# A new written-out order for five engines, and other queues for three early loads, in a fused spectral-filter and MLP kernel

## The chip, the cores and the metric

The kernel runs on one core of a Trainium2 chip. The metric is the device time of one execution in microseconds (us), lower is better. The profile is of one execution of the kernel before the change.

## What is computed

The input x is 2048 rows of 640 bf16 values. It is normalised along its rows (mean and variance, no scale), and two branches work on the normalised xn; their results are added to x.

```python
xn = (x - mean(x)) / sqrt(var(x) + 1e-5)
A  = irfft2(rfft2(xn) * (w_r + 1j * w_i))            # 2048 x 640
B  = gelu(xn @ w1 + b1) @ w2 + b2                    # 640 -> 1536 -> 640
out = x + A + B
```

Branch A is done with matrix products against cosine and sine tables; branch B is two dense layers. Both are work for TensorE.

## The kernel before

**Tiling.** The 2048 rows are 16 chunks of 128. Chunks are normalised one by one: two statistics instructions each on VectorE (line 651), their aggregation (653), the power -0.5 on GpSimd (655), the subtract-and-scale on VectorE (673). A normalised chunk is needed twice. Transposed, it is the right-hand side of the first dense layer: chunks 0 to 3 are transposed by TensorE against an identity matrix (692) and copied out of PSUM, chunks 4 to 15 by a DMA transpose issued by SyncE (680). Folded (two chunks at a time, "a pair": lines 704 and 708, VectorE), it is the left-hand side of the first spectral step, five matmuls a chunk against the table `gtab` (line 715), whose result is copied to `XV` (720) by ScalarE or VectorE.

**First dense layer.** The rows are taken in seven blocks, `BLOCKS = [(0, 1), (1, 1), (2, 2), (4, 2), (6, 2), (8, 4), (12, 4)]` (first chunk, number of chunks). For each block there are 12 slices of the hidden width, each of five matmuls (128 columns of x per chunk of the block), issued as a group of three and a group of two (lines 736 to 739), then one GELU on ScalarE (742) that empties the PSUM bank. W1 comes in three parts by slices, `W1P = [(0, 3), (3, 7), (7, 12)]`: slices 0 to 2, 3 to 6, 7 to 11. So a slice of block 1 with number 8 can only start when the third part of W1 has landed.

**The rest.** Then come the spectral steps B (against `etab`), C (`mtab`), the filter products on VectorE (809, 813), D (`ntab`), a DMA transpose back (834), E (`getab`) and the last step against `htab` (918) that is added into the same PSUM bank as the second dense layer (899), VectorE's addition of x (920) and the store (923). The second dense layer is 12 times 640 columns per chunk. For the chunks in `KEEP` it is done early and set aside by an addition on VectorE (911); for the others late. x and b2 are brought together in SBUF by a copy on ScalarE (887) and an accumulating DMA of GpSimd (905). All these matmuls are issued by the helper at line 536, so the profile tells them apart by tile names: `ps<-xnT,W` is the first dense layer, `ps<-W,gT` the second, `ps<-gtab,T` the first spectral step, `ps<-warm` matmuls on zeros that are issued to keep TensorE busy (42 at the start, 12 more later; `WARM`).

**Order.** The operations are numbered in the order in which the source creates them, and `ORDER` holds, for each engine (`sp`, `pe`, `act`, `dve`, `pool`), the list of its operations in the order in which it issues them. An engine runs its list strictly in order and waits at each entry for the semaphores of what that entry reads. `schedule()` walks the lists with a model of durations and of DMA landing times; with the lists given, what it decides is the PSUM bank or SBUF slot of each buffer, by the modelled times. For a DMA it computes a landing time:

```python
331  done = max(t + ring.lead, free[e] - dur + ring.lead, dma_free) + n * ROW_NS[size] / 1e3
338  o.end = done + TAIL + (LAG if 8.0 < t < 60.0 and o.engs[0][0] != "pool" and size != 256 else 0.0)
```

PSUM has eight banks. First-layer slices use banks 4 to 7, steps B, C, D and E use 0 to 3, the first spectral step takes three free banks of all.

**The loads at the start**, in the source:

```python
585  load_x(0, 1)
586  load(ident[:], const["I"], B_id, (8, 256), q="pool", prio=96, late=1.25)
587  load_x(1, 1)
588  load(b1t[:], b1v, B_b1, (1, 256), q="act", prio=410)
589  load_w1(0, q="act")
590  K.op([("act", 1.3)], 390, lambda e, _: e.preload_act_table(ACT.Gelu_apprx_tanh), ...)
591  load_w1(1)
592  load_x(2, 2)
593  load_w1(2)
```

**Numbers that the text uses** (the list entry, before / after, where the two differ because the start of the source or the number of copies at line 720 differs):

| operation | number before | number after |
|---|---|---|
| load of identity, of b1, of W1 part 0 | 9, 11, 12 | 10, 11, 13 |
| table load on ScalarE | 13 | 9 |
| load of x chunk 0, of x chunk 1 | 8, 10 | 8, 12 |
| W1 part 1, x chunks 2 and 3, W1 part 2, `gtab` | 14, 15, 16, 17 | the same |
| x chunks 4-5, 6-7, 8-9, 10-11, 12-13, 14-15 | 18, 19, 20, 24, 25, 28 | the same |
| b2, `getab` | 27, 50 | the same |
| W2 quarter 0, quarter 2, `mtab` | 23, 29, 32 | the same |
| DMA transposes of chunks 4 to 11 | 149 151 162 164 175 177 188 190 | the same |
| block 1 slice 8, first group | 290 | 289 |
| first spectral step of chunks 4 and 5 | 158, 159 | 158, 159 |
| first slice of block 3 (chunks 4 and 5) in the list | 353 | 343 |
| first part of the second layer, chunk 0 | 605 | 604 |

Of the kernel before, what the change touches and what calls it, by code (L numbers as in the profile page):

```python
# [9 lines left out]
ACT = mybir.ActivationFunctionType  # L10
# [77 lines left out]
HOLD = 0.3  # L88


def mm_us(n):
    return max(n / 2400.0 + 0.0027, 0.0265)

# [23 lines left out]
class Pool:  # L117
# [31 lines left out]


ORDER = {
    "sp": """8 10 14 15 16 17 18 27 50 46 24 20 19 25 23 149 151 30 45 162 164 42 28 29 38 175 177 31 188 190 36 32
26 37 33 40 41 39 217 47 34 48 49 44 219 202 43 204 35 521 522 523 520 544 545 546 51 547 570 568 569 571 595 594
593 592 621 658 648 638 612 694 675 710 720 685 730 756 765 747 782 798 791 805""",
    "pe": """7 52 112 114 115 236 230 231 120 233 118 237 234 245 246 248 249 275 276 284 285 269 270 278 279 239 242 243 240 272 266 273
# [8 lines left out]
728 760 761 754 762 745 763 785 786 787 780 792 793 788 789 794 795 796 799 800 801 802 803""",  # L164
    "act": """11 12 13 53 116 232 121 238 235 247 250 277 286 271 280 244 241 274 268 292 256 253 134 137 283 301 265 130 328 131 322 307
# [3 lines left out]
566 563 574 573 587 457 460 466 478 475 463 469 757 597 598 481 472 624 783 748 660 661 696 732 733 767""",  # L169
    "dve": """0 54 55 56 59 58 111 60 113 117 122 123 119 66 63 62 65 64 67 124 126 125 132 135 127 138 139 69 70 72 73 71  # L170
# [5 lines left out]
662 664 665 697 698 693 699 779 701 700 674 735 768 734 709 736 737 719 769 684 770 729 772 755 771 764 746 781 790 797 804""",  # L176
    "pool": """3 1 2 9 4 57 61 68 75 82 89 96 5 103 22 21 6 110 604 630 677 650 739 640 667 774 712 722 614 784 749 758
687 703""",
}


# [17 lines left out]

ROW_NS = {256: 26, 384: 22, 512: 27, 640: 33, 642: 70, 768: 37, 1024: 47, 1280: 56, 1600: 68, 2560: 103, 4096: 160, 10272: 750, "acc": 152}  # L200
TAIL = 0.9
LAG = 1.6


LAT = {"pe": 0.2, "dve": 0.125, "act": 0.16, "pool": 0.12}
# [2 lines left out]
class Sched:  # L208
# [37 lines left out]

    def schedule(self):
        free = {e: 0.75 for e in self.engines}
        dma_free = 0.0
# [29 lines left out]
        while left:  # L279
            best = None  # L280
            for e in self.engines:
                cands = []
                for o in [p for p in pend[e] if p is fixed[e][len(self.order[e])]] if fixed and len(self.order[e]) < len(fixed[e]) else pend[e]:
# [17 lines left out]
                    t = max(r, free[e])  # L301
# [7 lines left out]
                t0 = min(c[0] for c in cands)  # L309
# [3 lines left out]
                t, o = min(near, key=lambda c: (-c[1].prio, c[1].seq))  # L313
# [13 lines left out]
            if o.nbytes:  # L327
                n, size = o.rows
                ring = rings[e]
                free[e] = ring.issue_end(t, dur, n)  # L330
                done = max(t + ring.lead, free[e] - dur + ring.lead, dma_free) + n * ROW_NS[size] / 1e3
                if e == "pool" and size == 256:
                    done = t + ring.lead + 0.6
                    dma_free += n * ROW_NS[size] / 1e3
                else:
                    dma_free = done
                ring.held.append((done, n))
                o.end = done + TAIL + (LAG if 8.0 < t < 60.0 and o.engs[0][0] != "pool" and size != 256 else 0.0)
            else:
                o.end = t + dur + LAT[e]  # L340
            for b in o.writes:
# [60 lines left out]
    def emit(self, es, last):  # L402
# [40 lines left out]
PRIO = {"hps": 30.0, "gelu": 46.5, "pb": 53.0, "pc": 64.0, "filt": 77.5, "ipc": 53.5, "eps": 47.0, "fin": 46.5}  # L443
AHEAD = 1
# [4 lines left out]
FOLD = (1.3, 1.8, -3.7, 28.8, -1.2, 39.3, 36.8, -1.2)  # L449
GP = (-43.0, 20.0, 8.0, 14.0, -28.0, 2.0, -14.0)  # L450
G1 = 0
WAVE = (0, 4, 0, 0, 0, 1, 0, 4, 2, 2, 3, 0, 2, 1, 1, 2)
WARM = (42, 12)


def bass_parallel_sum__spectral_gfnet__dense_activation_gelu__prompt_kernel(
# [12 lines left out]
    const = {k: nc.inline_tensor(_bf16_bits(v.reshape(128, -1)), name=f"c_{k}").ap().bitcast(BF) for k, v in T.items()}  # L469
# [4 lines left out]
    b1v = B_b1.rearrange("(c p) -> c p", p=128)  # L474
    b2v = B_b2.rearrange("(o e) -> o e", o=1)

    K = Sched(nc, ["sp", "pe", "act", "dve", "pool"])
    with ExitStack() as es:
# [11 lines left out]
        ident = sb("ident", [128, 128])  # L490
# [7 lines left out]
        b1t = sb("b1t", [NFC, 128])  # L498
# [31 lines left out]
        def load(dst, src, buf, rows, after=(), q="sp", issue=0.46, prio=400, gate=(), late=0.0):  # L530
            return K.op([(q, 0.7 if q == "pool" else issue)], prio, lambda e, _: e.dma_start(dst, src), writes=[buf], after=after, rows=rows, gate=gate, late=late)  # L531
# [35 lines left out]
        B_id, B_b1, B_b2b = Buf("ident"), Buf("b1t"), Buf("b2")  # L567
# [22 lines left out]
        K.op([("act", 1.3)], 390, lambda e, _: e.preload_act_table(ACT.Gelu_apprx_tanh), writes=[Buf("table")], gate=[K.ops[-1]])  # L590
        load_w1(1)
        load_x(2, 2)
        load_w1(2)
# [64 lines left out]
        for pair in range(8):  # L658
# [10 lines left out]
            for n in range(2):  # L669
# [107 lines left out]
        for P in range(4):  # L777
# [69 lines left out]
        for gi, (c0, n) in enumerate(GROUPS):  # L847
# [20 lines left out]
            for i in range(n):  # L868
# [94 lines left out]
```

## Time and profile before

| | |
|---|---|
| median of 3 runs | 150.71 us (149.53 to 151.38) |
| profiled execution | 150.96 us, of which the span from first to last instruction 148.9 us |
| TensorE busy / weight loads | 140.9 us (95%) / 92.4 us |
| VectorE, ScalarE, GpSimd busy | 109.0, 85.8, 23.0 us |
| granted TensorE clock | 1.00 |
| DMA | 23.68 MB, mean 159 GB/s |

"Busy" is the union of the instructions' spans, and matmuls overlap in it, so a busy TensorE may still wait for weights. The waits view names what ended an idle stretch of an engine; the DMA view gives, for each kind of load, the time from issue to landing; the timeline merges neighbouring instructions of one kind (xN), its first column being the start in us, the second the length. The profiled time is 2.0 us longer than the span and 0.25 us above the median.

### The profile page before, as it was taken

The page shows a single profiled execution, that of the slowest core. Times are in us where ns is not written, and L with a number is a line of the kernel's source. Part 1 is how long each engine was busy: PE and PEld are TensorE (multiplying, and loading weights), DVE is VectorE, ACT ScalarE, POOL GpSimd, SP SyncE. Part 2 cuts the span into 40 slices and gives each one's busy share as a digit, 9 for nine tenths or more (in the row PEclk, how much of TensorE's full clock was granted, in tenths as well). Part 3 has the DMA queues.
Part 4 walks back from the last instruction along what each step waited for, and adds up shares of the span by engine and source line. Part 5 has one row for each costly group of instructions (what it writes and reads, how often), then busy time and mean ns, then how long its engine had stood idle before and what let it go on. Part 6 is the DMA issues. An engine that isn't in the chain of part 4 may idle for free.

```text
span 148.9 us, 4190 instructions
## 1 busy us (share of the span) xinstructions
PE 140.9 (95%) x1755; PEld 92.4 (62%) x1772; DVE 109.0 (73%) x232; ACT 85.8 (58%) x159; POOL 23.0 (15%) x38
## 2 busy tenths in 40 slices
PE   7599989999979999999999999999999999999993
PEld 7599979989537554436654544554447656665572
DVE  1699799999843369759945967796102999997992
ACT  3179998899957869889655442303378640350000
POOL 3302220305200027100240002020020380000000
PEclk9999999999999999999999999999999999999999
DMA  4999999898999948904939664944624099521243
GB/s 121 342 390 317 357 102 209 209 237 201 270 177 166 173 86 176 255 13 99 158 61 164 124 165 92 89 87 92 131 45 88 4 226 262 189 76 44 88 144 127
DMA packets 32122, 23.68 MB, mean 159 GB/s; under 512 B 20440, under 2 KB 28760, under 8 KB 31976
## 3 DMA queue, kind: packets, MB, share of 16 engines
q1 hardware_dynamic: 29024, 17.32, 53.2%
q0 software_dynamic: 2400, 5.61, 17.1%
q10 hardware_dynamic: 680, 0.49, 1.1%
q8 instruction: 14, 0.23, 0.7%
q14 instruction: 4, 0.03, 0.1%
HBM read 13.58 MB, written 2.62 MB: 109 GB/s over the span
## 4 chain that ended last, share of the span: by engine, by line
PE 78%; DMA 7%; SPq 5%; ACT 4%; DVE 2%; issue 2%
PE ps L536 78%; DMA X<-in_A_x_dram 7%; SPq L531 5%; ACT gT L742 2%; ACT XV L547 1%; DVE stats L651 1%; DVE T L708 1%; ACT X L887 0%; DVE T L704 0%; DVE W L920 0%; DVE mv L653 0%
## 5 line engine op out<-in xcount | busy, mean ns | idle before, releaser
L536 PE MATMUL ps<-W,gT 128*128 128x128 bf16 (+3 forms) x380 | 54.8, 292 | 2.6 <-issue 1.1
L536 PE MATMUL ps<-xnT,W 128*128 128x256 bf16 (+2 forms) x420 | 57.1, 288 | 0.0
L536 PEld LDWEIGHTS ps<-W,gT 128*128 128x128 bf16 x396 | 29.8, 98 | 24.0 <-issue 2.2
L536 PEld LDWEIGHTS ps<-xnT,W 128*128 128x128 bf16 x420 | 34.8, 98 | 15.4 <-issue 1.2
L742 ACT ACTIVATE gT<-ps,b1col 128x256 bf16<-128x256 f32 (+2 forms) x84 | 37.9, 508 | 9.2 <-PE ps L536 9.0
L651 DVE BATCH_NORM_STATS2 stats<-X 128x6 f32<-128x320 bf16 x32 | 13.9, 475 | 3.3 <-DMA X<-in_A_x_dram 3.3
L905 POOL DMA_DIRECT2D X<-in_A_x_dram x8 | 7.0, 1126 | 51.4 <-DMA Wf<-in_A_w_i_dram 15.3
L859 DVE TENSOR_TENSOR Wf<-Wf 128x960 bf16<-128x960 bf16 (+1 forms) x12 | 7.1, 595 | 9.7 <-ACT Wf L547 9.5
L547 ACT ACTIVATE Wf<-ps 128x960 bf16<-128x960 f32 (+1 forms) x9 | 7.6, 880 | 11.2 <-PE ps L536 11.0
L809 DVE TENSOR_TENSOR T<-Y,Wf 128x1288 bf16<-128x1288 bf16 x16 | 12.4, 825 | 1.3 <-ACT Y L547 1.3
L547 ACT ACTIVATE Y<-ps 128x644 bf16<-128x644 f32 x11 | 7.5, 705 | 6.4 <-PE ps L536 6.4
L547 ACT ACTIVATE XV<-ps 128x512 bf16<-128x512 f32 (+2 forms) x12 | 9.7, 830 | 2.5 <-PE ps L536 2.5
L655 POOL TENSOR_TENSOR rstd<-mv,mhalf 128x2 f32<-128x2 f32 (+1 forms) x9 | 6.3, 704 | 29.6 <-DVE mv L653 24.5
L905 POOL DMA_DIRECT2D xnT<-in_A_x_dram x8 | 7.3, 1296 | 17.4 <-DMA XV<-U 9.6
L547 ACT ACTIVATE U<-ps 128x512 bf16<-128x512 f32 (+1 forms) x10 | 3.8, 434 | 9.3 <-PE ps L536 9.3
L547 ACT ACTIVATE Xb<-ps 128x960 bf16<-128x960 f32 (+1 forms) x7 | 7.6, 1108 | 2.7 <-PE ps L536 2.7
L708 DVE TENSOR_TENSOR T<-T 128x512 bf16<-128x512 bf16 (+1 forms) x32 | 8.3, 306 | 0.1
L920 DVE TENSOR_TENSOR W<-ps,xnT 128x640 bf16<-128x640 f32 (+2 forms) x10 | 6.8, 690 | 2.1 <-PE ps L536 1.8
L548 DVE CAST Xb<-ps 128x960 bf16<-128x960 f32 (+1 forms) x5 | 5.8, 1169 | 2.8 <-PE ps L536 2.8
L536 PE MATMUL ps<-getab,XV 32*128 32x160 bf16 (+1 forms) x128 | 7.5, 241 | 0.0
L548 DVE CAST Y<-ps 128x644 bf16<-128x644 f32 x5 | 4.1, 827 | 4.4 <-PE ps L536 4.4
L536 PEld LDWEIGHTS ps<-getab,XV 32*128 32x128 bf16 (+1 forms) x128 | 6.5, 146 | 1.3
(51 smaller groups left out, 134.8 us busy)
## 6 DMA issues: line engine op xcount, KB each, us to landing
X<-in_A_x_dram POOLq DMA_DIRECT2D x8, 320.0 KB, 4.0
xnT<-in_A_x_dram POOLq DMA_DIRECT2D x8, 320.0 KB, 5.3
out_dram<-W SPq DMA_DIRECT2D x15, 160.0 KB, 1.8
X<-in_A_x_dram SPq DMA_DIRECT2D x7, 320.0 KB, 9.7
W<-in_B_w_dram SPq DMA_DIRECT2D x4, 480.0 KB, 6.2
Wf<-in_A_w_i_dram SPq DMA_DIRECT2D x6, 160.5 KB, 6.3
Wf<-in_A_w_r_dram SPq DMA_DIRECT2D x6, 160.5 KB, 5.3
W<-in_B_w_dram SPq DMA_DIRECT2D x1, 800.0 KB, 8.8
```

The source lines that it names most:

```text
L531: return K.op([(q, 0.7 if q == "pool" else issue)], prio, lambda e, _: e.dma_start(dst, src), writes=[buf], after=after, rows=rows, gate=g ...
L536: ins = e.matmul(o_, lhsT=lw, rhs=rh, start=st, stop=sp_, skip_group_check=True)
L547: return e.activation(dst(), src(), ACT.Copy, scale=scale)
L548: return e.tensor_copy(dst(), src())
L651: st_op[c] = K.op([("dve", 0.393)], pr, lambda e, _, c=c, h=h: e.bn_stats(stats[:, c, 6 * h:6 * h + 6], view(X, c * D + H2 * h, [[1, H2]]) ...
L655: K.op([("pool", 0.65)], 500, lambda e, _, a=a, b=b: e.tensor_tensor(out=rstd[:, a:b], in0=mv[:, a:b, 1], in1=mhalf[:, a:b], op=ALU.pow), ...
L708: ring_ops.append(K.op([("dve", dve_us(4 * w, 2))], pr, lambda e, _, op=op, x1v=x1v, xfv=xfv, o_=o_, o0=o0, o1=o1, w=w: e.tensor_tensor(ou ...
L742: K.op([("act", act_us(128 * nt, 1))], pr + PRIO["gelu"] + GP[bi], lambda e, _, c0=c0, nt=nt, fc=fc, hps=hps: e.activation(gT[:, fc, 128 * ...
L809: filt_ops.append(K.op([("dve", dve_us(4 * KP, 2))], pr, lambda e, _, k=k, Y=Y, TB=TB, pair=pair: e.tensor_tensor(out=view(TT, TB.slot * 8 ...
L859: K.op([("dve", dve_us(320 * n, 2))], pr + 2, lambda e, _, k=k, op=op, yo=yo, y2=y2, n=n: e.tensor_tensor(out=view(Wf, Y2 + y2.slot * 3 * ...
L905: xo_ops[c] = K.op([("pool", 0.9)], 51 - c / 20, lambda e, _, c=c, xov=xov: e.dma_start(xov(0, D), xv[:, c, :], accum_op=ALU.add), reads=[ ...
L920: K.op([("dve", dve_us(w))], 95, lambda e, _, os_=os_, fps=fps, o0=o0, w=w, xov=xov, base=base: e.tensor_tensor(out=view(W1, OST + os_.slo ...
```

## The change

Four things. (1) The loads: the identity is issued by ScalarE instead of GpSimd, behind b1 and the activation-table load; W1 part 0 is issued by SyncE behind x chunks 0 and 1 instead of by ScalarE; W1 parts 1 and 2 stay with SyncE. (2) The model of landing times: `LAG` becomes a table by issue time, the DMA transposes (40 rows of 256) are modelled to land after the last landing of any earlier DMA, and a small load on ScalarE gets a short fixed time. (3) All five lists of `ORDER` are new, with the settings that go with them: `KEEP` has nine chunks instead of ten, the copies at line 720 are split otherwise (`XASPLIT`), the first string of zero matmuls has 38 instead of 42, the accumulating DMAs wait for other transposes (`WAVE`). (4) The order of steps B, C and D (`CHAIN`) is changed in a few places. No operation is computed differently. The diff, cut:

```diff
+def lag(t, size):
+    if size == 256 or size == "acc":
+        return 0.0
+    if t >= 16.0 and size in (642, 10272):
+        return 0.3
+    return ([0.0] + [v for t0, v in LAG if t >= t0])[-1]
...
-    "sp": """8 10 14 15 16 17 18 27 50 46 24 20 19 25 23 149 151 30 45 162 164 42 28 29 38 175 177 31 188 190 36 32
-26 37 33 40 41 39 217 47 34 48 49 44 219 202 43 204 35 521 522 523 520 544 545 546 51 547 570 568 569 571 595 594
+    "sp": """8 12 13 14 15 16 17 18 19 29 32 20 23 25 149 151 24 28 43 164 162 175 41 177 188 190 27 35 38 30 31 42
+26 48 44 37 46 39 36 47 40 201 215 203 217 34 49 45 51 33 520 519 50 521 522 543 546 544 545 567 568 570 569 594
...
-    "pe": """7 52 112 114 115 236 230 231 120 233 118 237 234 245 246 248 249 275 276 284 285 269 270 278 279 239 242 243 240 272 266 273
-267 290 291 254 255 251 252 133 263 281 136 128 264 299 282 300 129 320 326 327 308 317 321 305 306 318 145 311 312 309 144 293
-294 335 336 302 260 261 314 303 332 287 288 333 315 159 329 330 158 257 323 258 324 353 354 350 351 347 348 341 342 368 359 365
+    "pe": """7 52 115 112 114 118 120 229 232 235 236 265 230 268 233 271 266 272 269 238 239 274 275 283 284 280 277 281 278 244 241 242
+245 247 248 289 290 259 260 250 256 257 134 286 137 251 287 129 128 292 304 293 322 305 325 326 146 145 316 323 301 328 302 317
+329 331 332 313 314 253 254 307 308 295 296 262 263 334 298 319 320 310 299 335 311 158 159 343 337 344 349 338 350 367 358 355
...
-    "act": """11 12 13 53 116 232 121 238 235 247 250 277 286 271 280 244 241 274 268 292 256 253 134 137 283 301 265 130 328 131 322 307
+    "act": """11 9 10 53 116 121 237 231 234 267 270 273 240 276 285 282 279 243 246 249 291 261 258 135 288 252 132 131 130 294 306 327
...
-    "dve": """0 54 55 56 59 58 111 60 113 117 122 123 119 66 63 62 65 64 67 124 126 125 132 135 127 138 139 69 70 72 73 71
-74 142 143 141 140 148 150 80 77 76 79 153 152 78 81 155 154 157 156 163 161 91 87 83 166 165 84 94 167 86 168 169
+    "dve": """0 55 54 58 56 59 60 111 117 113 119 123 122 126 124 125 63 62 65 66 64 67 127 133 136 139 140 138 142 143 144 141
+69 72 70 73 71 74 77 76 148 150 79 78 153 152 80 83 84 155 81 156 157 154 161 86 87 163 85 88 165 166 97 169
...
-    "pool": """3 1 2 9 4 57 61 68 75 82 89 96 5 103 22 21 6 110 604 630 677 650 739 640 667 774 712 722 614 784 749 758
+    "pool": """1 2 3 5 57 61 68 75 82 89 96 103 22 21 110 4 6 603 721 639 675 665 629 701 738 711 613 685 748 649 773 757
...
-LAG = 1.6
+LAG = ((1.6, 1.1), (3.9, 2.8), (16.0, 1.6), (60.0, 0.0))
...
-                done = max(t + ring.lead, free[e] - dur + ring.lead, dma_free) + n * ROW_NS[size] / 1e3
-                if e == "pool" and size == 256:
-                    done = t + ring.lead + 0.6
+                turn = size == 256 and n == 40
+                done = max(t + ring.lead, free[e] - dur + ring.lead, dma_last if turn else dma_free) + n * ROW_NS[size] / 1e3
+                dma_last = max(dma_last, done + lag(t, size))
+                if e == "act":
+                    done = t + ring.lead + 0.5
                     dma_free += n * ROW_NS[size] / 1e3
...
-                o.end = done + TAIL + (LAG if 8.0 < t < 60.0 and o.engs[0][0] != "pool" and size != 256 else 0.0)
+                o.end = done + TAIL + lag(t, size)
...
-CHAIN = "b1 b0 c00 c01 b2 c10 d01 c11 d00 b3 b4 d11 c21 d10 c20 b5 c31 d21 d20 c30 d30 d31".split()
-XASPLIT = ["01 234", "01 234", "01234", "01234", "01234", "01 234", "01 23 4", "01 234"]
-KEEP = (0, 2, 3, 4, 5, 6, 9, 10, 11, 14)
+CHAIN = "b1 b0 c01 c00 b2 c10 d01 c11 d00 b4 b3 d10 d11 c20 c21 b5 c30 d20 d21 c31 d30 d31".split()
+XASPLIT = ["01 23 4", "01234", "01234", "01234", "01234", "01234", "0123 4", "01 23 4"]
+KEEP = (0, 2, 3, 5, 6, 8, 9, 10, 11)
...
-WAVE = (0, 4, 0, 0, 0, 1, 0, 4, 2, 2, 3, 0, 2, 1, 1, 2)
-WARM = (42, 12)
+WAVE = (0, 3, 0, 0, 2, 0, 0, 4, 0, 2, 0, 2, 4, 2, 2, 3)
+WARM = (38, 12)
...
-        load(ident[:], const["I"], B_id, (8, 256), q="pool", prio=96, late=1.25)
+        K.op([("act", 1.3)], 420, lambda e, _: e.preload_act_table(ACT.Gelu_apprx_tanh), writes=[Buf("table")])
+        load(ident[:], const["I"], B_id, (8, 256), q="act", prio=410)
+        load(b1t[:], b1v, B_b1, (1, 256), q="act", prio=405)
         load_x(1, 1)
-        load(b1t[:], b1v, B_b1, (1, 256), q="act", prio=410)
-        load_w1(0, q="act")
-        K.op([("act", 1.3)], 390, lambda e, _: e.preload_act_table(ACT.Gelu_apprx_tanh), writes=[Buf("table")], gate=[K.ops[-1]])
+        load_w1(0)
         load_w1(1)
         load_x(2, 2)
         load_w1(2)
```

More of the change, by code (lines that the diff above doesn't have):

```diff
@@ L151 @@
 ORDER = {
-    "sp": """8 10 14 15 16 17 18 27 50 46 24 20 19 25 23 149 151 30 45 162 164 42 28 29 38 175 177 31 188 190 36 32
-26 37 33 40 41 39 217 47 34 48 49 44 219 202 43 204 35 521 522 523 520 544 545 546 51 547 570 568 569 571 595 594
-593 592 621 658 648 638 612 694 675 710 720 685 730 756 765 747 782 798 791 805""",
-    "pe": """7 52 112 114 115 236 230 231 120 233 118 237 234 245 246 248 249 275 276 284 285 269 270 278 279 239 242 243 240 272 266 273
[8 rows of a table removed]
-728 760 761 754 762 745 763 785 786 787 780 792 793 788 789 794 795 796 799 800 801 802 803""",
-    "act": """11 12 13 53 116 232 121 238 235 247 250 277 286 271 280 244 241 274 268 292 256 253 134 137 283 301 265 130 328 131 322 307
[3 rows of a table removed]
-566 563 574 573 587 457 460 466 478 475 463 469 757 597 598 481 472 624 783 748 660 661 696 732 733 767""",
-    "dve": """0 54 55 56 59 58 111 60 113 117 122 123 119 66 63 62 65 64 67 124 126 125 132 135 127 138 139 69 70 72 73 71
[5 rows of a table removed]
-662 664 665 697 698 693 699 779 701 700 674 735 768 734 709 736 737 719 769 684 770 729 772 755 771 764 746 781 790 797 804""",
-    "pool": """3 1 2 9 4 57 61 68 75 82 89 96 5 103 22 21 6 110 604 630 677 650 739 640 667 774 712 722 614 784 749 758
-687 703""",
+    "sp": """8 12 13 14 15 16 17 18 19 29 32 20 23 25 149 151 24 28 43 164 162 175 41 177 188 190 27 35 38 30 31 42
+26 48 44 37 46 39 36 47 40 201 215 203 217 34 49 45 51 33 520 519 50 521 522 543 546 544 545 567 568 570 569 594
+593 592 591 620 656 611 637 647 692 683 673 755 764 709 719 746 729 780 789 796 803""",
+    "pe": """7 52 115 112 114 118 120 229 232 235 236 265 230 268 233 271 266 272 269 238 239 274 275 283 284 280 277 281 278 244 241 242
[8 rows of a table added]
+775 707 717 776 783 727 777 784 790 744 791 778 785 792 786 787 793 794 797 798 799 800 801""",
+    "act": """11 9 10 53 116 121 237 231 234 267 270 273 240 276 285 282 279 243 246 249 291 261 258 135 288 252 132 131 130 294 306 327
[3 rows of a table added]
+562 612 565 566 575 648 576 586 590 480 589 468 462 477 471 465 596 474 622 658 659 781 695 694 772 731 732 767""",
+    "dve": """0 55 54 58 56 59 60 111 117 113 119 123 122 126 124 125 63 62 65 66 64 67 127 133 136 139 140 138 142 143 144 141
[5 rows of a table added]
+696 646 697 691 698 682 672 699 734 733 735 736 754 766 769 763 768 708 718 771 728 770 745 779 788 795 802""",
+    "pool": """1 2 3 5 57 61 68 75 82 89 96 103 22 21 110 4 6 603 721 639 675 665 629 701 738 711 613 685 748 649 773 757
+782""",
 }
@@ L248, in schedule @@
         free = {e: 0.75 for e in self.engines}
-        dma_free = 0.0
+        dma_free = dma_last = 0.0
         rings = {"sp": Ring(1.05, 140), "act": Ring(1.05, 140), "pool": Ring(1.7, 200)}
@@ L442 @@
         "eps": [(0, 4)], "fin": [(4, 8), (0, 4)], "fps": [(4, 8)], "tps": ANY, "aps": ANY}
-PRIO = {"hps": 30.0, "gelu": 46.5, "pb": 53.0, "pc": 64.0, "filt": 77.5, "ipc": 53.5, "eps": 47.0, "fin": 46.5}
-AHEAD = 1
-CHAIN = "b1 b0 c00 c01 b2 c10 d01 c11 d00 b3 b4 d11 c21 d10 c20 b5 c31 d21 d20 c30 d30 d31".split()
-XASPLIT = ["01 234", "01 234", "01234", "01234", "01234", "01 234", "01 23 4", "01 234"]
-KEEP = (0, 2, 3, 4, 5, 6, 9, 10, 11, 14)
-HOME = tuple(sorted((KEEP + tuple(c for c in range(16) if c not in KEEP))[-8:], key=lambda c: (c not in KEEP, c)))
-FOLD = (1.3, 1.8, -3.7, 28.8, -1.2, 39.3, 36.8, -1.2)
-GP = (-43.0, 20.0, 8.0, 14.0, -28.0, 2.0, -14.0)
-G1 = 0
-WAVE = (0, 4, 0, 0, 0, 1, 0, 4, 2, 2, 3, 0, 2, 1, 1, 2)
-WARM = (42, 12)
+PRIO = {"hps": 23.0, "gelu": 27.0, "pb": 67.5, "pc": 50.5, "filt": 84.0, "ipc": 36.0, "eps": 80.0, "fin": 28.5}
+AHEAD = 3
+CHAIN = "b1 b0 c01 c00 b2 c10 d01 c11 d00 b4 b3 d10 d11 c20 c21 b5 c30 d20 d21 c31 d30 d31".split()
+XASPLIT = ["01 23 4", "01234", "01234", "01234", "01234", "01234", "0123 4", "01 23 4"]
+KEEP = (0, 2, 3, 5, 6, 8, 9, 10, 11)
+HOME = tuple(sorted((KEEP + tuple(c for c in range(16) if c not in KEEP))[-8:], key=lambda c: (c not in KEEP, c)))
+FOLD = (1.3, 1.8, -3.2, 66.3, 45.3, 69.8, 50.8, 17.3)
+GP = (-81.0, 42.0, 4.0, 72.0, -32.0, 6.0, -9.0)
+G1 = 1
+WAVE = (0, 3, 0, 0, 2, 0, 0, 4, 0, 2, 0, 2, 4, 2, 2, 3)
+WARM = (38, 12)
 def bass_parallel_sum__spectral_gfnet__dense_activation_gelu__prompt_kernel(
```

26 rows, old and new, of the table ORDER are left out of this document.

## The prediction

> **What bounds the kernel now.** I read the page first, then TensorE's idle time, then the timeline around each idle stretch, then the loads.
>
> ```profile
> span 148.9 us, 4190 instructions
> PE 140.9 (95%) x1755; PEld 92.4 (62%) x1772; DVE 109.0 (73%) x232; ACT 85.8 (58%) x159; POOL 23.0 (15%) x38
> ...
> PE   7599989999979999999999999999999999999993
> ...
> PEclk9999999999999999999999999999999999999999
> DMA  4999999898999948904939664944624099521243
> ```
>
> TensorE works in nearly every fortieth from the third on, at full clock. All its work stays under the change (the same matmuls but for four zero ones), so the question is only how long it waits. The waits of TensorE, and the timeline rows that follow them:
>
> ```profile
> PE ps L536 <- DMA ident<-c_I: 1.6, 1, 1.6
> PE ps L536 <- issue: 1.1, 7, 0.2
> PE ps L536 <- ACT gT L742: 1.1, 1, 1.1
> ...
> PE ps L536 <- DVE T L708: 0.4, 1, 0.4
> ```
>
> ```profile
> 6.53 0.18 PE L536 MATMUL ps<-ident,b1t 12*128 12x12 bf16 x1 [1.60 <-DMA ident<-c_I]
> ...
> 7.61 0.61 PE L536 MATMUL ps<-xnT,W 128*128 128x128 bf16 x8
> ...
> 8.50 4.09 PE L536 MATMUL ps<-xnT,W 128*128 128x128 bf16 x69
> ...
> 12.60 0.29 PEld L692 LDWEIGHTS ps<-ident,T 128*128 128x128 bf16 x5 [0.18 <-ACT gT L742]
> ...
> 18.36 1.67 DVE L651 BATCH_NORM_STATS2 stats<-X 128x6 f32<-128x320 bf16 x4 [0.96 <-DMA X<-in_A_x_dram]
> ...
> 21.97 0.23 PE L536 MATMUL ps<-gtab,T 128*128 128x128 bf16 x1 [0.38 <-DVE T L708]
> ...
> 43.27 1.57 PE L536 MATMUL ps<-W,gT 128*128 128x128 bf16 x11 [1.07 <-ACT gT L742]
> ```
>
> Useful work starts at 7.61. After it there are three waits: at 12.6 for normalised chunk 2 (its scale ends at 12.48), at 21.97 for the folds of chunks 4 and 5, which are late because x chunks 6-7 came at 18.3 and VectorE stood 0.96 in front of them, and at 43.27 for a GELU that must empty a PSUM bank. A 128-column matmul is shown 0.22 long but its successor starts 0.056 after it (69 in 4.09), so a gap costs 0.16 more than it shows: 0.38 is 0.54, 1.07 is 1.23, and the one at 12.6 (a gap of the weight loads only) 0.20. Together **1.97 us**. From 43 on the chain of waits is TensorE alone, to 146.54; the tail of 2.4 us after it (last addition, store) stays. So the change can win about 2 us there, plus what it wins at the start.
>
> **The start.** The loads, KB and median us from issue to landing:
>
> ```profile
> X<-in_A_x_dram SPq DMA_DIRECT2D x7, 320.0 KB, 9.7
> ...
> W<-in_B_w_dram SPq DMA_DIRECT2D x1, 800.0 KB, 8.8
> W<-in_B_w_dram SPq DMA_DIRECT2D x1, 640.0 KB, 6.7
> ...
> W<-in_B_w_dram ACTq DMA_DIRECT2D x1, 480.0 KB, 6.1
> ...
> ident<-c_I POOLq DMA_DIRECT2D x1, 32.0 KB, 5.2
> ```
>
> and of ScalarE's timeline
>
> ```profile
> 1.83 1.28 ACT L590 ACT_TABLE_LOAD   x1 [1.83 <-issue]
> ```
>
> Identity: now issued by GpSimd at 1.31, landed 6.5, and TensorE waits for it. After: ScalarE issues b1 (0.74 to 1.36), loads its table (1.28), then issues the identity at about 2.7. No row shows a small load on that queue: below, x chunk 0's 2.4 us on an idle SyncE queue gives 5.1; above, GpSimd's own 5.2 gives 7.9. I take 3.0, nearer the low end since it is small and ScalarE's queue holds nothing else: 5.7. Then b1's matmul, 12 zero matmuls (0.67), ten transposes (0.56), a copy (0.4): the first slice at about 7.1. VectorE is no later: three statistics, two aggregations, one statistics and two scales from 3.15 on put chunk 0 at 5.7 and chunk 1 at 6.3. The 38 zero matmuls are four fewer at 0.056 (0.2 us), and they end before the identity anyway.
>
> But this gain goes nowhere. Blocks 0 and 1 have only 2 x 7 slices that do without W1's third part (slices 0 to 6). A slice is 5 x 0.056 = 0.28, so 14 take 3.9 and end at 11.0; entry 289 (slice 8, block 1) then waits for that part. Before, it was issued at 2.69 and landed 8.8 later, 11.5, and entry 290 started at 11.59 at once. After, W1 part 0 stands ahead of it on SyncE, so it is issued 0.5 later. By latency it lands at 12.0; by bytes at 11.5, since the same 2.6 MB (x 0 to 3 and all W1) must land first and the DMA row is at nine tenths from the second fortieth on. I take 11.5 (range 10.8 to 12.0): the start is worth 0.1 us, and x chunks 2 and 3 arrive as before. By the Trainium skill ("DMA: Bandwidth & Descriptors", section "Issuing engines are not separate DMA queues") loads of all issuing engines share the same 16 DMA engines and a second issuer saves only issue time. By that rule the move of part 0 shifts nothing here and the sum stays; by the latency row alone it would be 0.5 us worse.
>
> What does change: before, 13 slices and the two transposes of chunk 1 by TensorE (0.28) stood ahead of that point after 7.61; after, 14 slices. One slice, **0.28 us**, is work moved into time that was idle.
>
> **After the third part of W1: TensorE's list against VectorE's and SyncE's.** Up to entry 158 TensorE has 10 slices of blocks 0 and 1 (2.8), two chunk transposes (0.55), four spectral steps (4 x 0.28) and all 12 slices of block 2 (256 columns, 0.109 a matmul from 23 in 2.67: 0.545 a slice, 6.5): 11.0 us, so it gets there at 22.5. VectorE, from chunk 2's scale at 12.03 (it still waits for rstd, and the transpose of chunk 2 then costs 0.1): two scales 0.71, two folds 0.8, the copy of chunk 3 that VectorE takes over (0.45, not before 13.6), then folds 0.9, six statistics 2.4, aggregations 0.24, chunk 4's scale at 17.6 and, after chunk 5's and more of the same, the folds of chunks 4 and 5 at 21.9. x chunks 6-7 are now the load behind 4-5 and land near 14.3 instead of 18.3, so the 0.96 is gone. The wait at 21.97 goes, with 0.6 to spare.
>
> What is late next is the DMA transpose. Entry 343 starts block 3 at 23.1, right after the two spectral steps; before, three slices (1.4 us) of blocks 0 and 2 stood between. That cover is used up. Block 3 needs chunks 4 and 5 transposed:
>
> ```profile
> L680 SPq DMA_TRANSPOSE xnT<-T x12: 1204/1308/2527, 17.1 to 49.0; - x12
> ...
> DMA to landing us min/median/max: 4.2/4.9/6.8
> ```
>
> Chunk 4's scale ends at 18.0, 0.95 later than before (two statistics of chunk 6 and a copy are ahead of it now), so its transpose is issued at 18.0 and chunk 5's at 19.4. Landing: with the minimum 4.2 at 23.6, with the median 24.3, with the maximum 26.2; an empty queue (2.7 for the later transposes to `XV`) gives 22.1. Fewer loads stand ahead at that time than before (x 10-11, b2 and `getab` are moved behind), so 4.5: 23.9, **0.8 us** (0 to 3.1). Behind these two SyncE now holds x 10-11 and 14-15 (issued by 23), then chunks 7 and 6: issued near 25.2, landed 29.7, needed at 30.5. Chunks 8 to 11 land near 35.6, needed at 37. VectorE needs x 10-11 at 26.4, they land near 26: slack there 1 us.
>
> The GELU wait of 1.23: ScalarE has as much to do ahead of step B as before (24 + 34 + 6 GELUs for 23 + 34 + 3), but VectorE takes parts of the last copies to `XV`, and the second layer's first part, which found no free pair of banks at 43.27, comes behind step C. Bank waits can appear elsewhere: 0 to 1.2, I take **0.3**. Late half: filter loads end with three behind the last transpose, some 3 us before VectorE's first products hold up step D; steps E stand 1.6 to 3.5 us apart and their banks are emptied in 1 to 2: 0 to 0.5, I take **0.2**. One set-aside addition less (0.74 on VectorE) is off the path. The landing model issues nothing; it moves only banks.
>
> **Sum.** Span 148.9 - 1.97 - 0.28 - 0.1 + (0.1 + 0.8 + 0.3 + 0.2) = 147.95; the profiled execution is 2.06 over its span: 150.0. It lies 0.25 above the median, so **149.7** against 150.71, 0.7% less.
>
> **Rivals.**
> Small waits at many tight joints as large in all as the old ones (2.35 instead of 1.4): **150.7**, nothing won. For it: margins of 0.1 to 0.3 us at many bank changes. Against: TensorE lost next to nothing there before.
> A clean order (0.2 of waits): **148.6**; with W1's third part 0.7 earlier as well 147.9. For it: VectorE and ScalarE have slack from 30 on. Against: the missing cover at block 3.
> Slower, by one mechanism: the transpose of chunk 5 at its maximal 6.8 lands at 26.2, block 3 waits 3.1 instead of 0.8: **152.1**. It passes no change when the landing is after 24.9 (5.5 from issue).
> The identity comes no sooner: at GpSimd's latency, 7.9, the first slice is at 9.5, 14 slices end at 13.4 instead of 11.5, 1.9 more: **151.7**. It begins to cost from 6.2 on.
>
> **Chances.** Forecast 0.45, nothing won 0.18, clean 0.16, late transpose 0.13, late identity 0.08. The range takes in the clean order with an early W1 and the late transpose: 147.9 to 152.2. A measurement of this kernel tells about 2% from no change: faster than 147.7 needs the clean case and more, 0.05; slower than 153.7 needs two of the mishaps, 0.05; within, 0.90.
>
> **What would show it.** Right: identity landed before 6.2, first `ps<-xnT,W` near 7.1, a new wait of TensorE near 11 for W1's third part; no 0.96 on VectorE before statistics; no wait for T at 22; a wait for a transpose at 23. Wrong: a wait of over 2 us at block 3, first slices after 8, or idle stretches of TensorE over 1 us after 30.

## The result, and the profile after

The changed kernel takes 149.82 us (median of 22 runs, 148.43 to 152.47) against 150.67 for the kernel before beside it (22 runs): a ratio of 0.9934, 95% interval 0.9909 to 0.9959. That is 1.0 us (0.6 to 1.4) less: real, and far inside the 2% that count as no change. An unchanged copy of it, measured later on another chip, gave 149.66 us and 0.9931 (0.9905 to 0.9957). The profiled execution took 150.22 us, its span is 148.2. The ratios here and below leave out executions that took over 1.5% longer than the fastest of their kernel; the medians hold them all.

The page of the kernel after, span, TensorE and the slices:

```profile
span 148.2 us, 4179 instructions
...
PE 141.3 (95%) x1749; PEld 92.4 (62%) x1768; DVE 106.1 (72%) x225; ACT 88.1 (59%) x164; POOL 22.4 (15%) x37
...
PE   7998999999999999999999999999999999999992
...
PEclk9999999999999999999999999999999999999998
DMA  4999859897999997498975607364364703890234
```

TensorE is as full as before; the whole result is again a matter of short waits. The waits of TensorE in the kernel after (what was waited for: us in total, times, longest):

```profile
PE ps L546 <- issue: 1.5, 9, 0.2
PE ps L546 <- DVE warm L562: 1.0, 1, 1.0
PE ps L546 <- DVE W L930: 0.6, 1, 0.6
PE ps L546 <- ACT gT L752: 0.6, 2, 0.4
```

The 1.6 for the identity, the 1.1 at 43 us and the 0.4 for the folds at 22 are gone from the list. New in it is `W L930`, the last additions before the stores. The 1.5 put down to `issue` is mostly no wait: 1749 matmul records stand against 1768 weight loads, and where a record is missing the row behind it seems to start late. In a_again, with 1768 of both, that line is not there. Now the start, in the timeline of TensorE (start, duration, in brackets the idle time ahead of the row):

```profile
0.99 3.74 PE L546 MATMUL ps<-warm 128*128 128x128 bf16 x38 [0.99 <-DVE warm L562]
4.67 0.18 PE L546 MATMUL ps<-ident,b1t 12*128 12x12 bf16 x1
4.78 0.84 PE L546 MATMUL ps<-warm 128*128 128x128 bf16 x12
5.67 1.05 PE L702 MATMUL ps<-ident,T 128*128 128x128 bf16 x10
6.64 1.15 PE L546 MATMUL ps<-xnT,W 128*128 128x128 bf16 x16
7.97 3.37 PE L546 MATMUL ps<-xnT,W 128*128 128x128 bf16 x54 [0.18 <-ACT gT L752]
11.73 1.16 PE L546 MATMUL ps<-xnT,W 128*128 128x128 bf16 x18 [0.39 <-ACT gT L752]
12.74 0.44 PE L702 MATMUL ps<-ident,T 128*128 128x128 bf16 x5
```

Useful work starts at 6.64 instead of 7.61, but the first slice that needs the third part of W1 stands at 11.73, before at 11.59: the whole 0.97 us is spent in waits ahead of it. The reason is in the loads (KB, median us from issue to landing); the 800 KB one is the third part, issued by SyncE at 3.35, so landed at 11.6:

```profile
W<-in_B_w_dram SPq DMA_DIRECT2D x1, 800.0 KB, 8.2
...
ident<-c_I ACTq DMA_DIRECT2D x1, 32.0 KB, 2.7
```

The page blames a GELU for the 0.39 at 11.73; that GELU ended at 11.61 and the part landed at 11.60, so one execution can't say which of the two it was. Several can. For eleven kernels' profiled executions, read one instruction at a time (us):

| kernel (see below) | third part landed | first slice on it | last matmul ends | from that slice to the end |
|---|---|---|---|---|
| before | 11.46 | 11.59 | 146.53 | 134.94 |
| b_loads | 11.70 | 11.83 | 145.21 | 133.38 |
| b_x67 | 11.34 | 11.74 | 145.50 | 133.76 |
| after | 11.60 | 11.73 | 145.84 | 134.11 |
| a_again (after, unchanged) | 11.13 | 11.27 | 144.73 | 133.46 |
| a_os8 | 11.86 | 11.99 | 144.71 | 132.72 |
| a_os8_b | 12.28 | 12.41 | 145.46 | 133.05 |
| a_os8_w50 | 11.72 | 11.85 | 145.26 | 133.41 |
| a_zero48 | 12.06 | 12.72 | 145.66 | 132.94 |
| a_w50 | 11.65 | 12.39 | 145.22 | 132.83 |
| a_oldloads | 11.97 | 14.11 | 147.01 | 132.90 |

In seven of the eleven the slice starts 0.13 or 0.14 us after the landing, whatever GELU came then: the load sets it. In b_x67 and the last three the slices ahead of it were themselves late. After it the kernel after and its variants need 132.7 to 134.1; the difference is for the most part their later waits, as the rows of the end below show for two of them.

The end, in the timeline of the kernel after, VectorE and TensorE:

```profile
58.84 0.83 DVE L819 TENSOR_TENSOR T<-Y,Wf 128x1288 bf16<-128x1288 bf16 x1 [1.41 <-DMA Wf<-in_A_w_i_dram]
...
62.99 0.52 PE L546 MATMUL ps<-Z,ntab 32*32 32x320 bf16 x32 [0.25 <-issue]
...
143.89 1.45 DVE L930 TENSOR_TENSOR W<-ps,xnT 128x640 bf16<-128x640 f32 x3 [0.76 <-DMA out_dram<-W]
144.77 1.00 PE L546 MATMUL ps<-W,gT 128*128 128x160 bf16 x12 [0.58 <-DVE W L930]
```

At 58.84 VectorE gets a filter part 1.41 us late, and works without a pause from there to 62.89, where its copy of a result of step C frees the PSUM bank; step D starts behind it at 62.99, 0.32 late: 0.62 us after the start of the matmul ahead of it, where a_again has 0.31. At 143.89 VectorE waits for an output staging slot whose store (issued 139.82) lands at 143.81; TensorE loses 0.74. Another 0.28, which shows only from start to start, lies at 70.22 in a step B. That is 1.34 us of waits behind the third part in this execution, and 0.68 in a_again (0.13 at 74.74, 0.55 at 143.65). Without them the two need 132.77 and 132.78.

### The profile page after: what moved, and what is told of

It reads as the page before. It is cut to its first block, busy times and chain, and to the rows that moved or that the text cites. A ratio compares the mean times of both kernels' runs of the same rounds, so it can differ in the third digit from the quotient of the medians.

```text
span 148.2 us, 4179 instructions
## 1 busy us (share of the span) xinstructions
PE 141.3 (95%) x1749; PEld 92.4 (62%) x1768; DVE 106.1 (72%) x225; ACT 88.1 (59%) x164; POOL 22.4 (15%) x37
## 4 chain that ended last, share of the span: by engine, by line
PE 86%; DMA 4%; DVE 4%; issue 3%; ACT 1%; POOL 1%; DVEq 0%
PE ps L546 85%; DMA out_dram<-W 3%; DVE W L930 2%; DMA X<-in_A_x_dram 2%; ACT gT L752 1%; DVE stats L661 1%; POOL rstd L665 1%; PE ps L702 1%; DVE Wf L558 1%; DVE T L683 0%; DVE Wf L869 0%; DVE mv L663 0%; DVEq L429 0%
## 5 line engine op out<-in xcount | busy, mean ns | idle before, releaser
L546 PE MATMUL ps<-xnT,W 128*128 128x256 bf16 (+2 forms) x420 | 58.0, 288 | 0.6 <-ACT gT L752 0.6
L546 PE MATMUL ps<-W,gT 128*128 128x128 bf16 (+3 forms) x379 | 55.7, 292 | 2.2 <-issue 1.1
L557 ACT ACTIVATE Xb<-ps 128x960 bf16<-128x960 f32 (+1 forms) x8 | 8.8, 1124 | 6.2 <-PE ps L546 6.2
L915 POOL DMA_DIRECT2D X<-in_A_x_dram x8 | 7.5, 1568 | 28.3 <-DMA Wf<-in_A_w_i_dram 20.4
L558 DVE CAST Wf<-ps 128x640 bf16<-128x640 f32 (+1 forms) x3 | 2.8, 931 | 10.9 <-PE ps L546 10.9
L921 DVE TENSOR_TENSOR X<-ps,X 128x640 f32<-128x640 f32 x8 | 6.5, 820 | 3.4 <-PE ps L546 3.2
L557 ACT ACTIVATE U<-ps 128x512 bf16<-128x512 f32 (+1 forms) x12 | 4.6, 434 | 7.3 <-PE ps L546 7.3
L557 ACT ACTIVATE XV<-ps 128x1280 bf16<-128x1280 f32 (+2 forms) x11 | 8.8, 831 | 0.0
L930 DVE TENSOR_TENSOR W<-ps,xnT 128x640 bf16<-128x640 f32 (+2 forms) x10 | 6.7, 686 | 2.7 <-PE ps L546 1.9
L683 DVE TENSOR_SCALAR T<-X,mv,rstd 128x640 bf16<-128x640 bf16 x16 | 6.8, 443 | 2.1 <-POOL rstd L665 1.6
```

The lines of the kernel that those rows point to most:

```text
L546: ins = e.matmul(o_, lhsT=lw, rhs=rh, start=st, stop=sp_, skip_group_check=True)
L557: return e.activation(dst(), src(), ACT.Copy, scale=scale)
L558: return e.tensor_copy(dst(), src())
L915: xo_ops[c] = K.op([("pool", 0.9)], 51 - c / 20, lambda e, _, c=c, xov=xov: e.dma_start(xov(0, D), xv[:, c, :], accum_op=ALU.add), reads=[ ...
L921: kept_ops.append(K.op([("dve", dve_us(D))], 30, lambda e, _, kps=kps, xov=xov: e.tensor_tensor(out=xov(0, D), in0=psb(kps.slot, [[1, D]]) ...
L930: K.op([("dve", dve_us(w))], 95, lambda e, _, os_=os_, fps=fps, o0=o0, w=w, xov=xov, base=base: e.tensor_tensor(out=view(W1, OST + os_.slo ...
```

## The experiments

Kernels named b_ are variants of the kernel before, a_ of the one after. Edits in the lists move numbers of loads or steps within one engine's order.

**b_x67: x chunks 6-7 earlier, alone.** In before, load 19 moves right behind x 4-5:

```
-"sp": 8 10 14 15 16 17 18 27 50 46 24 20 19 25 23 149 151 ...
+"sp": 8 10 14 15 16 17 18 19 27 50 46 24 20 25 23 149 151 ...
```

> The kernel before with one move: the load of x chunks 6-7 is issued right behind that of chunks 4-5 (as after the change) instead of behind b2, getab, x 10-11 and 8-9. Theory: the idle 0.96 of VectorE before statistics at 18.4 goes, and with it TensorE's wait of 0.54 for the folds at 22; the two other waits (0.20 and 1.23) stay: 0.3 to 0.6 us faster than before, ratio near 0.997. Rival (the 0.96 was only cover, and the wait for the next load or for the transposes of chunks 4 and 5 takes its place): 0.0, and a new wait of VectorE for x 8-9 or 10-11 in the trace.

150.15 us, ratio 0.9963 (0.9929 to 0.9997): 0.55 us faster (0.05 to 1.1). VectorE no longer stands idle before the statistics of chunk 6, and the wait at 22 us is gone, as expected. Not as expected, the two other waits did not stay: neither the 0.20 at 12.6 nor the one at 43 us is in this execution, and a new one came, 0.59 from start to start at 37.60 (waits of TensorE):

```profile
PE ps L536 <- DMA xnT<-T: 0.4, 1, 0.4
```

**a_x67late: the same part undone.** In after, load 19 goes back behind x 8-9:

```
-"sp": ... 17 18 19 29 32 20 23 25 149 151 ...
+"sp": ... 17 18 29 32 20 19 23 25 149 151 ...
```

> After with the load of x blocks 6 and 7 put back behind the load of x blocks 8 and 9 in SyncE's queue, so that it lands near 18.2 us, as in before (18.34), in place of 15.90. Theory: VectorE's statistics of chunk 6 (16.95 us in the profile of after) then wait 1.3 us, everything behind them on VectorE too; the last fold of chunks 4 and 5 ends near 23.4 in place of 22.11, TensorE's step on it stands at 22.76, so a wait of 0.6 to 0.7 us comes back there, and the kernel is 0.4 to 0.7 us slower than after: a ratio to before of 0.996 to 0.998. Rival: the folds have slack enough and TensorE shows no wait near 22 to 24 us: the ratio stays at 0.993. A second rival: the later normalisation of chunks 4 and 5 also delays their DMA transposes past the start of block 3 (23.3), and the loss is over 1 us: a ratio of 1.0 or more.

150.79 us, ratio 0.9986 (0.9945 to 1.0028): some 0.8 us slower than after by the ratios, whose intervals just overlap. Its timeline, VectorE and then TensorE:

```profile
17.99 0.89 DVE L661 BATCH_NORM_STATS2 stats<-X 128x6 f32<-128x320 bf16 x2 [1.26 <-DMA X<-in_A_x_dram]
...
23.10 0.73 PE L546 MATMUL ps<-gtab,T 128*128 128x128 bf16 x10 [0.50 <-DVE T L718]
```

1.26 on VectorE and 0.50 shown, 0.67 in all, on TensorE: the theory's 1.3 and 0.6 to 0.7. (This execution took 153.22 us, with further waits behind 70 us; only the stretch ahead of them is read.) Chunk 5's transpose, 0.95 later too, landed at 23.35, still ahead of block 3, which starts at 23.67: the second rival's mechanism did not come. Put in or taken out, the earlier load of x 6-7 is worth about half a microsecond or more by the middle values, half of the change's gain; the intervals allow much less.

**b_loads: the new order of the first loads, alone.** In before, identity by ScalarE, W1's part 0 by SyncE (their numbers move in the lists with them):

```
-  load(ident[:], const["I"], B_id, (8, 256), q="pool", prio=96, late=1.25)
+  load(ident[:], const["I"], B_id, (8, 256), q="act", prio=96)
-  load_w1(0, q="act")
+  load_w1(0)
```

> The kernel before with the early loads of the change alone: the identity by ScalarE behind b1, W1 part 0 and the table load, W1 part 0 by SyncE behind x chunks 0 and 1; all orders else as before. Theory: the first slice starts 0.5 to 0.9 earlier, TensorE then stands that much longer before W1's third part at 11.6, and the time is 0.0 to 0.2 us less. Rival (an earlier start is an earlier end): 0.7 to 0.9 us less, ratio near 0.994.

150.15 us, ratio 0.9988 (0.9953 to 1.0023): nothing that can be told. The timeline of TensorE shows why:

```profile
6.86 0.61 PE L536 MATMUL ps<-xnT,W 128*128 128x128 bf16 x8 [0.34 <-DMA W<-in_B_w_dram]
...
8.71 2.95 PE L536 MATMUL ps<-xnT,W 128*128 128x128 bf16 x50 [0.57 <-ACT gT L742]
11.83 1.00 PE L536 MATMUL ps<-xnT,W 128*128 128x128 bf16 x15 [0.17 <-DMA W<-in_B_w_dram]
...
41.74 1.79 PE L536 MATMUL ps<-W,gT 128*128 128x512 bf16 x12
```

0.75 earlier at the first slice, and 0.24 later at the slice on the third part, which here TensorE is shown to wait for. The last row is the second layer's first part: the lists there are those of before, and it starts without a wait, and so do the folds' steps at 22 us.

**a_oldloads: the old loads in the new order.**

```
-  load(ident[:], const["I"], B_id, (8, 256), q="act", prio=410)
+  load(ident[:], const["I"], B_id, (8, 256), q="pool", prio=410, late=1.25)
-  load_w1(0)
+  load_w1(0, q="act")
```

> The kernel after with the early loads as they were before: identity by GpSimd, W1 part 0 by ScalarE; all lists else as after. Theory: the first slice starts at 7.6 instead of 6.6, the 14 slices end at 11.5, W1's third part lands at 11.5 to 11.6 as it did, and the time is 0.0 to 0.2 us more than after's 149.8. Rival (the early loads are what the change gains): 0.8 to 1.0 us more, as slow as before.

150.54 us, ratio 0.9984 (0.9942 to 1.0027): about 0.75 us slower than after, nearer the rival. Timeline of TensorE:

```profile
6.67 0.19 PE L546 MATMUL ps<-ident,b1t 12*128 12x12 bf16 x1 [1.44 <-DMA ident<-c_I]
6.79 1.46 PE L546 MATMUL ps<-warm 128*128 128x128 bf16 x12
8.04 1.27 PE L702 MATMUL ps<-ident,T 128*128 128x128 bf16 x10
9.30 1.37 PE L546 MATMUL ps<-xnT,W 128*128 128x128 bf16 x15
```

The identity lands at 6.62, and the twelve zero matmuls behind it take 1.46 us instead of 0.84: TensorE issued a 128-column matmul every 107 ns here until 10.2 us, twice the 56 of later. The slice on the third part starts at 14.11, 2.1 after its landing. So the new order seems to need the early loads, though in the old order they bring nothing; the intervals of this run and of after overlap, and it says that weakly. How much of the 0.75 in the timed runs is the late identity and how much the slow rate of this one execution stays open.

**a_zero48: the slack of the start.** `WARM = (38, 12)` becomes `(38, 48)`, 36 zero matmuls more behind b1.

> The kernel after with 48 instead of 12 zero matmuls ahead of the first chunk's transposes: 36 more, 2.0 us more work for TensorE at the start. Theory: TensorE has about 1.0 us of waits between its first slice and W1's third part (0.35, 0.12 and 0.56 in the trace of after), so half is absorbed: 0.9 to 1.1 us slower than after, and the slice that needs the third part starts near 12.7. Rival (the start is on the path): 2.0 us slower than after. Second rival (the stretch to 22 has slack too): under 0.5.

150.52 us, ratio 0.9996 (0.9962 to 1.0029): 0.9 us slower than after, as expected.

```profile
4.66 2.85 PE L546 MATMUL ps<-warm 128*128 128x128 bf16 x48
...
8.27 1.07 PE L546 MATMUL ps<-xnT,W 128*128 128x128 bf16 x16 [0.20 <-ACT xnT L557]
```

The slice on the third part starts at 12.72 (12.7 expected), 0.66 after its landing: 2.0 us added, about 1 taken by the waits of the start.

**a_os8 and a_os8_b: eight staging slots.** `Pool(2), Pool(1), Pool(2), Pool(4)` becomes `... Pool(8)`; measured twice, the second time beside the copy of after.

> The kernel after with eight instead of four staging slots for the output stores. Theory: in the trace of after VectorE stands 0.76 at 143.1 because the addition for chunk 15 must wait until the store of an earlier chunk has landed (4.0 us after its issue), and TensorE stands 0.58 (0.74 from start to start) for the bank that this addition empties; with eight slots both go: 0.5 to 0.8 us faster than after's 149.8, ratio to before near 0.989. Rival (the late store is an accident of that one execution): 0.0 to 0.2.

149.49 us (148.84 to 149.74), ratio 0.9893 (0.9846 to 0.994).

> After with 8 output staging slots in place of 4, measured again beside an unchanged copy of after. Theory: the wait of 0.74 us at 144.77, in which VectorE waits for a slot that an old store still holds, is all that falls away: 0.4 to 0.8 us faster than the copy, a ratio to before 0.003 to 0.005 lower. Rival: the last piece is as late for another reason (VectorE's queue), and the two are equal within 0.2 us.

149.36 us (149.21 to 149.98), ratio 0.9935 (0.9912 to 0.9958); the copy a_again stood at 149.66 (148.49 to 151.38) and 0.9931.

> The kernel after, unchanged, so that the three variants below have it beside them on one chip. Both theories: a ratio to before of 0.991 to 0.996, a profiled span of about 148. What differs from one execution to the next is read here too: the moment from which the opening string of zero matmuls is issued every 56 ns instead of every 107 ns stood at 4.13 us in the profile of after and at 5.28 and 6.20 in two of its variants, although all three open with the same instructions.

The timeline of a_os8_b, VectorE and TensorE near the end, has no idle time where after had 0.76 and 0.58:

```profile
142.69 2.36 DVE L930 TENSOR_TENSOR W<-ps,xnT 128x640 bf16<-128x640 f32 x4
...
144.40 0.99 PE L546 MATMUL ps<-W,gT 128*128 128x160 bf16 x12
```

The wait is the staging slot's, then, and it goes. But beside the copy no gain is left: the 0.6 us of the first measurement was read against a run of after on another chip, and that theory falls. It is not a wait of every run's full size (0.55 in a_again), and removing it leaves the two equal within 0.3 us. No variant here beats the kernel after by more than can be measured.

**a_w50 and a_os8_w50: twelve zero matmuls more at the opening.** `WARM = (50, 12)`, with four and with eight slots.

> After with 50 zero matmuls in the opening string in place of 38. Twelve more are 0.66 us at 55 ns each, or 1.28 at 107 ns. Theory of the slack: TensorE waits 0.35, 0.12 and 0.56 us, 1.03 together, between its first slice and the first slice that needs W1's third part, so 0.66 us more of zeros costs nothing (within 0.2 us of the copy of after), where 36 more cost 0.9. Rival: each zero shifts the whole, 0.66 us slower, 0.0044 in the ratio.

149.81 us, ratio 0.9964 (0.9942 to 0.9985), against 0.9931 of the copy.

> Both edits together: 50 zero matmuls in the opening string and 8 staging slots. Theory: the slack takes the zeros, the slots give their 0.4 to 0.8 us: equal to the variant with 8 slots alone within 0.2 us, a ratio to before of about 0.989. Rival of the zeros that shift everything: 0.66 us slower than 8 slots alone, about 0.993.

149.84 us, ratio 0.9960 (0.9938 to 0.9983), against 0.9935 of a_os8_b. Both are 0.4 to 0.5 us slower than their partners: nearer the rival's 0.66 than the slack's nothing, though the intervals overlap. The two profiles show both: in a_os8_w50 the fast rate came at 3.7 us and the slice on the third part followed its landing by 0.13 (no cost); in a_w50 it came at 6.0, the 50 zeros took 5.30 us, and that slice was 0.74 behind the landing. The slack is there, but not in each execution.

**a_xfirst: two loads ahead of the DMA transposes.** In after, x 10-11 and 14-15 go ahead of the transposes of chunks 4 and 5:

```
-"sp": ... 20 23 25 149 151 24 28 43 ...
+"sp": ... 20 23 25 24 28 149 151 43 ...
```

> The kernel after with the loads of x 10-11 and 14-15 issued ahead of the transposes of chunks 4 and 5 again (as x 10-11 was before). Theory: a DMA transpose lands when what is queued ahead of it has landed; 0.66 MB more is ahead (2.0 us at 330 GB/s), so chunk 5's transpose lands near 24.2 instead of 22.4, block 3 (due at 23.3) waits about 0.9 us, and the kernel is 0.6 to 1.0 us slower than after. Rival (a transpose takes its 2.7 to 4.5 us from issue whatever is queued): same as after within 0.2.

150.01 us, ratio 0.9944 (0.9913 to 0.9975): 0.15 to 0.2 us slower than the 0.9934 and 0.9931 of after by the middle values, nothing that can be told. In the profile (an execution of 152.01 us, read here up to block 3 alone) chunk 5's transpose took 4.15 us instead of 2.7 and landed at 23.79, and block 3 waits for it (timeline of TensorE):

```profile
23.88 1.36 PE L546 MATMUL ps<-xnT,W 128*128 128x256 bf16 x11 [0.33 <-ACT gT L752]
```

0.33 shown, 0.50 in all; the row names a GELU, but the slice starts 0.09 after the transpose's landing. The mechanism is the theory's, the wait smaller than the 0.9 that it gave, and the timed runs don't show its cost.

**b_x67_gelu: the wait at 43 us, by hand.** In b_x67 the second layer's first part (605 to 608) moves from ahead of step B to behind it, with three other steps filling its place:

```
-"pe": ... 416 411 605 606 226 227 607 371 485 372 608 417 482 422 ...
+"pe": ... 416 411 417 371 372 226 227 485 482 605 606 607 608 422 ...
```

> The kernel before with x 6-7 behind 4-5, and with the second layer's first part (chunk 0) moved in TensorE's list from before the last two spectral steps to behind the first two steps B, three groups of first-layer slices taking its place. Theory: the waits of 0.54 and 1.23 both go, some of the latter comes back as a wait for the last folds near 42: 1.0 to 1.7 us faster than before, so the two waits are all that the change gains. Rival (the gain lies in the whole order, and other joints give it back): under 0.6 us faster.

153.29 us, ratio 1.0109 (1.0039 to 1.0179): slower. Timeline of TensorE:

```profile
45.70 1.31 PE L536 MATMUL ps<-etab,XV 128*128 128x160 bf16 x24 [0.95 <-DVE XV L548]
48.47 0.96 PE L536 MATMUL ps<-etab,XV 128*128 128x160 bf16 x16 [1.45 <-ACT Xb L547]
```

The moved part was what TensorE did while VectorE and ScalarE made the operands of step B; without it step B waits twice, 1.11 and 1.52 us from start to start. The theory of this move falls. Nor did it have a wait to remove: b_x67 shows none at 43 us, for a reason given in the next section.

## Why the prediction came out as it did

**Time.** 149.7 against 149.82 and 149.66: right. The main reason it gave, old waits of TensorE removed and smaller new ones in their place, is shown by experiment for one of the two large old waits, the one at 22 us. The other was misread, and not each size was right.

**Start.** Worth about nothing in the old order, as said: first slice at 6.64 (7.1 predicted, though the terms written there add to 7.4), third part's slice at 11.73 and 11.27 (11.5). b_loads, the loads alone, shows no gain. Taken out of the new order they seem to cost some 0.75 (a_oldloads), which the prediction did not see. The size of one term was off: the identity was to be issued at 2.7, behind the table load. ScalarE's rows in after:

```profile
1.41 1.28 ACT L596 ACT_TABLE_LOAD   x1 [1.41 <-PEq L958]
1.44 0.36 ACTq L541 DMA_DIRECT2D ident<-c_I  x1
```

It was issued while the table was loading, and landed 2.7 later at 4.1, not 5.7; that is ahead of the end of the 38 zero matmuls, which so set the start of what follows (4.67). Nor were the four zeros left out 0.056 us each, as the prediction has it: at the start they come one in 107 ns. That the move of W1's part 0 to SyncE would leave the third part's landing alone held: 11.46 before, 11.60 and 11.13 after, 11.70 in b_loads, while issue came 0.66 later. Over all runs it is 11.1 to 12.3 in ten executions with the new loads and 11.3 to 12.0 in four with the old. So the rule that the prediction cited from the Trainium skill ("DMA: Bandwidth & Descriptors", section "Issuing engines are not separate DMA queues") agrees with these runs.

**Waits removed, 1.97.** None of the three is in after. For the one at 22 us b_x67 and a_x67late show the cause, x 6-7, from both sides; in b_loads, where x 6-7 stayed late, VectorE stood 0.42 for it and TensorE not at all, since it came to that point 0.25 later.

The one at 43 us was misread twice. Its size: before shows twelve weight loads for the eleven matmuls of the row at 43.27.

```profile
43.03 1.49 PEld L536 LDWEIGHTS ps<-W,gT 128*128 128x128 bf16 x12 [1.32 <-ACT gT L742]
```

The first matmul, of 512 columns and 0.22 us, has no record: the row at 43.27 begins with the second. So the wait is 1.02, not 1.23, and the three waits are 1.76. Its cause: entry 605 waits for ScalarE's entry 421 and for all four quarters of W2, since `B_w2` is one buffer with four writers. Entry 421 ended at 41.44; the GELU that ended at 42.99, which the row names, is entry 412 behind it, and 605 does not wait for that. The last quarter of W2 was issued at 36.02,

```profile
W<-in_B_w_dram SPq DMA_DIRECT2D x1, 480.0 KB, 7.0
```

and landed at 42.97. In the trace TensorE's wait for its semaphore ends at 43.00. In b_loads and b_x67 the same load landed at 41.27 and 41.57, each 0.26 ahead of the part's first weight load, and the wait is not there. So no GELU and no bank was late: it was a load with little slack, late in one of the three executions that have this order there. After the change the part starts at 52.13 and that load lands at 45.67: here the new order did remove the risk, by the step the prediction named (the part comes behind step C) and not for its reason. How often before pays for that load in the timed runs is not shown.

So 1.97 was one execution's sum: b_loads needed 133.38 from the third part's slice to the end, against 134.94; the 1.56 between them is the two waits.

**One slice more ahead of the third part, 0.28.** Without its waits the old order needs 133.2 from that slice on, by three executions: 134.94 - 1.76, b_loads' 133.38 - 0.20, b_x67's 133.76 - 0.59. The new order needs 132.7 to 132.8 (132.72 in a_os8, which shows no wait there). That is 0.4 to 0.5, of which the slice is 0.28; where the rest lies was not traced.

**New waits, 1.4.** The sum came out (1.34 in the profile of after, 0.68 in its copy), its parts did not. The step that failed here is chunk 5's transpose: 0.8 was taken, with 4.5 us from issue to landing. Loads issued between 18 and 21 us in after, and TensorE's rows at block 3:

```profile
xnT<-T SPq DMA_TRANSPOSE x2, 3.1
```

```profile
22.76 0.72 PE L546 MATMUL ps<-gtab,T 128*128 128x128 bf16 x10
23.32 1.91 PE L546 MATMUL ps<-xnT,W 128*128 128x256 bf16 x16
```

Chunk 4's took 3.57, chunk 5's 2.73 (2.6 to 2.7 in eight more executions that keep these entries of SyncE's list): the last load ahead of them had landed at 20.3, the queue ran empty, and 22.40 is 0.9 before the need. The prediction had the empty queue's 2.7 in its bounds and saw fewer loads ahead, but stayed near the rows of before, behind loads. The cover it missed is indeed gone: with two loads put ahead (a_xfirst) the wait is there, 0.50. The GELU wait of 0.3 did not come. What came instead is the late half: 0.2 was taken for filters and banks, 0.32 and 0.28 measured, and the 0.74 at the last piece was in no term. That too small and too large cancelled, here and in the two terms above, is chance.

**Rivals.** Identity late, late transpose, and nothing won: ruled out, the last by the interval. The clean order (148.6) is what a_again's profiled execution would give without its waits: 149.18 - 0.68.

## What to carry to other kernels

Where one engine is full, find the one arrival behind which it never stands idle for long, here the third part of W1: what is gained ahead of it is lost in front of it, and only fewer bytes ahead of it or fewer waits behind it move the end. A load moved a few places in a queue can be worth about half of what five new lists win; ask which consumer stands idle for it and undo that one move. Before a wait is put into a sum, check in the kernel what the instruction waits for, and in a second execution whether the wait is there: the name in a row can be of something that only ended at that time. Price a DMA by what its queue holds when it is issued, not by the median of the same instruction in another order, and take no gain under 1% as real unless both versions ran side by side.

## What the runs showed of the hardware

From the same opening string of zero matmuls (twelve more in a_w50), the moment at which zero matmuls go from one in 107 ns to one in 56 varied between executions: 4.13 us in after, 3.83 in its copy, 5.28 in a_os8, 6.2 in a_xfirst, 6.0 in a_w50, 10.2 in a_oldloads (whose TensorE paused 1.4 us for the identity), while the granted clock in the profile's rows read full speed. The Trainium skill ("TensorE: Matmul & The Clock Gate", section "What's actually happening") describes a start at half rate until a free-running window of some 3.4 us has been busy; that it varies agrees, but it gives 500 ns either way, and these runs show over 2 us with like openings.
